# A transformer block with attention and MLP: other homes for the input tiles, other engine for a tile's statistics, and a finer first projection

## The chip, the core and the metric

The kernel runs on one core of a Trainium2 chip. The core has a matrix engine (TensorE, PE in the profile), a vector engine (VectorE, DVE), a scalar engine for activations (ScalarE, ACT), a general one (GpSimd, POOL) and a queue engine (SyncE, SP) from which this kernel issues all of its DMAs. On-chip memory is SBUF; TensorE writes into PSUM, eight banks of which hold 512 fp32 values in each of 128 partitions. The metric is the device time of one execution in microseconds (us). The kernel before took 1038.02 us in the median of three runs (1036.59 to 1038.26).

## The reference

The input x has 2048 rows of 1024 values (bf16). With xn = layernorm(x), the output is x + s * g, where s is an attention block on xn (32 heads of 32, no mask, no second layernorm) and g = silu of an MLP on xn that begins with a layernorm of its own:

```
xn = _layernorm(x, axis=-1)
s = _A_ref(xn, A_wqkv, A_wo)          # qkv = xn @ wqkv; softmax(q k^T / sqrt(32)) v; @ wo
g = _silu(_B_ref(xn, B_w1, B_b1, B_w2, B_b2))   # layernorm, @ w1 + b1, gelu, @ w2 + b2  (F = 3584)
return x + s * g
```

## The kernel before

**Tiling.** x is cut into 16 tiles of 128 rows, x0 to x15. Heads are taken in 8 groups of four (hg 0 to 7). For a group, queries are cut into 8 blocks of 256 (qb) and keys into 8 pairs of 128 (kp, 256 keys). One *unit* (`unit`, L830) is one (qb, kp): eight score matmuls (line L846, called S here), then two exps on ScalarE of 128x1024 values each (L855), then the products with V. 512 units make 1024 exps' worth of work, 1004 of them in the trace's main group. The MLP, the projections and the output product run on TensorE between the units.

**A planner writes the order.** Every operation is declared with its engine, an estimated duration, a priority and what it reads and writes. `_Plan.run` then plays the engines against each other with those estimates and fixes one order for each engine; `settle` adds the semaphore waits. On the chip each engine goes through its list strictly in order, so an instruction that waits holds up everything behind it on its engine. The planner's estimate of a DMA has one common bandwidth queue for SP. Among ready operations of an engine the smaller (priority, index) goes first. In one stretch of planned time, 60 to 90 us, a seed adds noise to some of these choices; the noise depends on the operation's index and on the time.

**The prologue** (first 60 us). For each tile: load (`load_x`, L626, on SP), statistics, rstd, normalised bf16 copy (`normalize`, L748, on DVE), and transposition into xnT, which the projections read.

- Statistics on DVE are two `bn_stats` of 512 values (L785), a `bn_aggr` (L787) and an add of eps (L792). For tile 1 (`AT = 1`) ScalarE does them in place of DVE, with two passes of 1024 values with accumulation (L769), followed by three tiny DVE operations (L772, L774, L777). rstd is a power on POOL (L794), one for each of tiles 0 to 3 and one for each later pair.
- Tiles 0 to 3 are transposed by TensorE (`tr_item`, L733) and copied out of PSUM by ScalarE (L737). Tiles 4 to 15 are transposed by DMA (L752, `DMA_TRANSPOSE xnT<-gw`), issued from SP.
- The normalised copies use four buffers in turn (xnb, in the trace `gw`). The loaded tiles use ten buffers (`NXS = 10`, in the trace `hT`): x0 to x9 are loaded at the start, x10 to x15 only after an earlier tile of the same buffer has been normalised. On SP their loads stand between the DMA transposes.
- The projections of head group 0 are `q_item(n)` and `k_item(n)`, one for each pair of tiles (2n, 2n+1): eight matmuls of 256 columns (L617), and a copy out of PSUM (Q by DVE, L712; K by ScalarE, L722). The first units need Q(0) and K(0); the order of the first units (`order0`) is (0,0), (0,1), (1,0), (1,1), (0,2), (1,2), (2,0), (2,1), (0,3) and so on, so four units, eight exps, can run with tiles 0 to 3, and the ninth exp needs K(2), that is tiles 4 and 5. Head group 0's V follows from `v_item` with the weights wv.
- While TensorE waits, the planner lets it run small matmuls on the identity (`filler`, L668).

Tile numbers t4, t5 and so on below mean the DMA transposes of those tiles.

## Time and profile before

| | us |
|---|---|
| median of three runs | 1038.02 |
| profiled execution, its own time | 1038.8 |
| span of the profiled execution, first to last instruction | 1037.0 |
| ScalarE busy | 1017.2 (98%) |
| TensorE busy | 1000.8 (97%) |
| VectorE busy | 940.6 (91%) |
| start of the first exp | 13.26 |
| last exp ends | 1026.3 |

The profiled time is 0.8 us above the median; 1.8 us of it lie outside the span. Busy times are sums of instruction durations; a TensorE that is busy need not be at its peak. An instruction's row ends in brackets with the idle time of its engine just before it and with what ended that idle time.

### The profile page before, as it was taken

The numbers are of one execution on the slowest core, as the hardware profiler recorded it, in microseconds if no ns is written. First come the engines' busy times: TensorE is split into PE (matmuls) and PEld (weight loads), VectorE is DVE, ScalarE is ACT, GpSimd is POOL, SyncE is SP. The second block draws the span as 40 slices with busy tenths as digits, with TensorE's granted clock in tenths as the row PEclk, the third lists the DMA queues.
The fourth block names the chain that finished last, engine by engine and source line by source line (L and its number), as shares of the span: only waits on it lengthen the run. The fifth ranks groups of instructions, "written<-read, shape, count | busy, mean of one in ns | idle before, by whom it ended". The sixth has DMA issues, their size and how long they took to land.

```text
span 1037.0 us, 31480 instructions
## 1 busy us (share of the span) xinstructions
PE 1000.8 (97%) x14096; PEld 638.6 (62%) x14161; DVE 940.6 (91%) x1308; ACT 1017.2 (98%) x1094; POOL 11.5 (1%) x21
## 2 busy tenths in 40 slices
PE   8999999999999999999999999999999999899997
PEld 6656557666766567666666676666666665664443
DVE  7658999999889999997899989998999889877898
ACT  6999999999999999999999999999999999999996
POOL 2200000000000000000000000000000000000000
PEclk9999999999999999999999999999999999999999
DMA  7994655635665658456447576565365762784421
GB/s 204 166 234 118 173 166 165 191 108 147 192 186 167 168 152 227 129 147 194 136 129 189 146 215 172 159 179 161 104 160 161 212 175 70 230 249 137 135 79 52
DMA packets 318199, 167.99 MB, mean 162 GB/s; under 512 B 56688, under 2 KB 306032, under 8 KB 318064
## 3 DMA queue, kind: packets, MB, share of 16 engines
q1 hardware_dynamic: 318064, 165.98, 58.0%
q8 instruction: 111, 1.82, 0.8%
q14 instruction: 24, 0.20, 0.1%
HBM read 146.55 MB, written 12.06 MB: 153 GB/s over the span
## 4 chain that ended last, share of the span: by engine, by line
ACT 85%; PE 10%; DMA 2%; DVE 2%; issue 1%; SPq 0%; POOL 0%
ACT P L855 78%; PE ps L617 6%; ACT ut L1037 5%; PE ps L612 3%; PE ps L846 2%; DMA xnT<-gw 1%; ACT gw L1064 1%; DMA w2r<-in_B_w_dram 1%; DVE stats L785 1%; DMA hT<-in_A_x_dram 0%; DVE gw L748 0%; DVE hT L1293 0%; DVE V L690 0%; DVE hT L1287 0%; DVE mv L787 0%
## 5 line engine op out<-in xcount | busy, mean ns | idle before, releaser
L855 ACT ACTIVATE P<-ps 128x1024 bf16<-128x1024 f32 x1004 | 937.4, 1236 | 3.6 <-PE ps L846 3.4
L872 DVE TENSOR_TENSOR PA<-P 128x2048 bf16<-128x2048 bf16 x175 | 212.3, 1216 | 38.3 <-ACT P L855 37.7
L617 PE MATMUL ps<-yT,w1r 128*128 128x256 bf16 x1792 | 228.5, 273 | 1.0 <-DVE hT L1022 0.7
L617 PE MATMUL ps<-w2r,hT 128*128 128x256 bf16 x1792 | 223.2, 273 | 0.5 <-DMA w2r<-in_B_w_dram 0.2
L846 PE MATMUL ps<-QKT 32*128 32x256 bf16 x4096 | 203.3, 273 | 13.8 <-ACT P L855 10.9
L886 DVE TENSOR_TENSOR PR<-PR,PA 128x2048 bf16<-128x2048 bf16 x175 | 211.6, 1210 | 1.2
L617 PEld LDWEIGHTS ps<-yT,w1r 128*128 128x128 bf16 x1792 | 164.1, 98 | 54.5 <-issue 29.3
L617 PEld LDWEIGHTS ps<-w2r,hT 128*128 128x128 bf16 x1792 | 163.4, 98 | 50.0 <-issue 31.3
L846 PEld LDWEIGHTS ps<-QKT 32*128 32x128 bf16 x4096 | 60.7, 92 | 144.3 <-ACT P L855 137.3
L612 PE MATMUL ps<-P,V 128*32 128x256 bf16 x4016 | 137.2, 274 | 0.3 <-issue 0.3
L617 PE MATMUL ps<-xnT,wqk 128*128 128x512 bf16 (+1 forms) x511 | 119.1, 360 | 6.5 <-DMA xnT<-gw 2.4
L612 PEld LDWEIGHTS ps<-P,V 128*32 128x32 bf16 x4016 | 95.0, 96 | 31.8 <-issue 22.5
L617 PE MATMUL ps<-wv,xnT 128*128 128x256 bf16 (+1 forms) x576 | 87.1, 285 | 0.5 <-DMA xnT<-gw 0.2
L617 PEld LDWEIGHTS ps<-xnT,wqk 128*128 128x128 bf16 x560 | 49.6, 98 | 53.3 <-issue 14.1
L1022 DVE TENSOR_TENSOR hT<-ps,b1T 128x512 bf16<-128x512 f32 x112 | 76.5, 683 | 1.8 <-PE ps L617 1.1
L872 DVE TENSOR_TENSOR PR<-P 128x2048 bf16<-128x2048 bf16 x61 | 74.1, 1214 | 0.4 <-ACT P L855 0.2
L617 PEld LDWEIGHTS ps<-wv,xnT 128*128 128x128 bf16 x576 | 52.4, 98 | 24.1 <-issue 11.4
L1037 ACT ACTIVATE ut<-ut 128x2048 bf16<-128x2048 bf16 (+1 forms) x32 | 61.0, 1906 | 0.0
L702 DVE CAST QKT<-ps 128x512 bf16<-128x512 f32 x58 | 39.6, 683 | 1.3 <-PE ps L617 0.9
L941 DVE STREAM_TRANSPOSE nt<-ps 128x256 f32<-128x256 f32 x64 | 28.4, 443 | 12.7 <-PE ps L612 12.5
L1039 DVE TENSOR_TENSOR hT<-ut,hT 128x2048 bf16<-128x2048 bf16 (+1 forms) x32 | 34.5, 1079 | 0.2
L1034 DVE TENSOR_TENSOR ut<-hT 128x2048 bf16<-128x2048 bf16 (+1 forms) x32 | 34.5, 1079 | 0.1
(96 smaller groups left out, 549.5 us busy)
## 6 DMA issues: line engine op xcount, KB each, us to landing
w1r<-in_B_w_dram SPq DMA_DIRECT2D x112, 512.0 KB, 4.2
w2r<-in_B_w_dram SPq DMA_DIRECT2D x128, 448.0 KB, 4.6
hT<-in_A_x_dram SPq DMA_DIRECT2D x20, 256.0 KB, 3.9
wqk<-in_A_wqkv_dram SPq DMA_DIRECT2D x16, 256.0 KB, 3.9
yst<-in_A_x_dram SPq DMA_DIRECT2D x16, 256.0 KB, 4.4
g_scratch<-gw SPq DMA_DIRECT2D x32, 128.0 KB, 3.9
o_scratch<-ot SPq DMA_DIRECT2D x56, 64.0 KB, 3.4
xnT<-o_scratch SPq DMA_DIRECT2D x7, 512.0 KB, 6.6
```

The costliest lines, as they stand in the source:

```text
L612: ins = e.matmul(dst(j), lhsT=lhsT(j), rhs=rhs(j), start=start, stop=stop, tile_position=(0, 32 * j), skip_group_check=True)
L617: return e.matmul(dst, lhsT=lhsT, rhs=rhs, start=start, stop=stop, skip_group_check=True)
L702: dve(lambda e: e.tensor_copy(QKT[sl][:, which, tq * 512:(tq + 1) * 512], bank(it.bank)), c_ps(512), [], [(nm, sl, 2 * tq), (nm, sl, 2 * t ...
L846: ins = e.matmul(bank(b0[j], kk * 256, (kk + 1) * 256), lhsT=QKT[sl][32 * j:32 * j + 32, 1, kb * 128:(kb + 1) * 128], rhs=QKT[sl][32 * j:3 ...
L855: x = act(lambda e, h=h: e.activation(Pt[pi][:, 2 * h:2 * h + 2].rearrange("p j k q -> p (j k q)"), ps[:, pr[h] * 1024:(pr[h] + 1) * 1024] ...
L872: return dve(lambda e: e.tensor_tensor(dst[:].rearrange("p u j q -> p (u j) q"), src[:].rearrange("p u j k q -> p (u j) k q")[:, :, 0, :], ...
L886: return dve(lambda e: e.tensor_tensor(fl3(pr), fl3(pr), fl3(PA[i]), op=ALU.add), c_b16(2048), [("PA", i), tok], [tok], 3.2)
L941: dve(lambda e: e.transpose(nt_t[:], bank(pv.bank, 256, 512)), c_ps(256) + 120, [], [("nt",)], prio, pv)
L1022: dve(lambda e: e.tensor_tensor(hT[:, hs], bank(it.bank).rearrange("p (k t) -> p k t", k=2), b1T[:, 2 * pi:2 * pi + 2].unsqueeze(2).to_bro ...
L1034: dve(lambda e: e.tensor_tensor(u_, x_, x_, op=ALU.mult), c_b16(n), hs_, [("ut", ui)], 3)
L1037: act(lambda e: e.activation(u_, u_, ACT.Tanh, scale=GC), c_acts(n), [("ut", ui)], [("ut", ui)], 1)
L1039: dve(lambda e: e.tensor_tensor(x_, u_, x_, op=ALU.mult), c_b16(n), [("ut", ui)] + hs_, hs_, 3)
```

## The change

All sixteen x tiles get homes of their own: x10 to x13 in the two PR buffers, x14 and x15 in the two yst buffers, both idle that early. All sixteen loads are issued one after another, right behind the first weights and ahead of wv. ScalarE takes the statistics of tile 3 too (`AT = (1, 3)`). Q(0) and K(0) are computed by one item, `qk_first`, in halves of 128 columns: first everything of tile 0, then tile 1 in two halves of the contraction, since tile 1's copy out of PSUM comes in two halves; K's half of it lands in PSUM bank 1. K(1) is cut into halves of 128 columns as well. While `qk_first` is open and waits, the planner may put a TensorE transposition between its matmuls; fillers are not planned while an item is open. The first load of the next head group's K weights now waits for the normalisation of tile 15 in place of tile 9; the MLP's first input loads, into yst, wait until tiles 14 and 15 have been normalised, in place of tile 11.

```diff
-        NTR, NWARM, NG0, AT = 4, 8, 3, 1
+        NTR, NWARM, NG0, AT = 4, 8, 3, (1, 3)
...
         xst = [h_flat[:, i * 1024:(i + 1) * 1024] for i in range(NXS)]
+        for i in range(2):
+            pr_flat = PR[i][:].rearrange("p u j q -> p (u j q)")
+            xst += [pr_flat[:, 0:1024], pr_flat[:, 1024:2048]]
+        xst += [yst_t[i][:] for i in range(2)]
...
-        XS = lambda t: ("xst", t % NXS)
+        XS = lambda t: ("xst", t)
...
         wk0 = load_qk(0, 1)
         wq0 = load_qk(0, 0)
-        for t in range(4, NXS):
+        for t in range(NTR, NT):
             load_x(t)
         load_v(0)
...
         def k_item(n):
             it = _Item("pro", 0.01 * n)
-            for dc in range(DC):
+            for lo, w in ((0, 128), (128, 128)) if n < 2 else ((0, 256),):
+                for dc in range(DC):
...
+        def qk_first():
+            it = _Item("pro", -0.001)
+            for lo, d0, d1 in ((0, 0, 8), (128, 0, 4), (128, 4, 8)):
+                for k, wi in ((0, wq0), (1, wk0)):
+                    for dc in range(d0, d1):
+                        def fn(e, b, dc=dc, lo=lo, k=k, wi=wi):
+                            return mm(e, bank(k or b, lo, lo + 128), wqk[wi][:, dc, :], xnT[:, dc, lo:lo + 128],
+                                      dc == 0 and lo == 0, dc == DC - 1)
+                        chunk(it, fn, Q128, [("xnT", lo // 128, dc), ("wqk", wi)], [("S", 0, 1)] if k else ())
...
-                if ts == (AT,):
+                if ts[0] in AT:
+                    a_ = ts[0]
                     for k, f, sc in ((0, ACT.Copy, 1.0 / D), (1, ACT.Square, D ** -0.5)):
...
-                    if t >= NXS:
-                        load_x(t, [first[2 * n - 5]])
...
-            wk = load_qk(hg, 1, [first[9]] if hg == 1 else ())
+            wk = load_qk(hg, 1, [first[NT - 1]] if hg == 1 else ())
...
-                    [("yst", t2)], rate=390.0, extra=[first[11]] if c == 0 else ())
+                    [("yst", t2)], rate=390.0)
...
+        for i in range(2):
+            after([("PR", i)], [XS(10 + 2 * i), XS(11 + 2 * i)])
+            after([("yst", i)], [XS(14 + i)])
```

In the planner, `pe_step` gets the rule for the inserted transposition:

```diff
+            tq, th = self.dense["tr"], heads["tr"]
+            if use is None and S["do"] is not None and th < len(tq) and tq[th].chunks[0].left == 0 and tq[th].chunks[0].ready <= t:
+                heads["tr"] += 1
+                tq[th].k = 1
+                S["mode"] = "d"
+                commit(tq[th].chunks[0], t)
+                return
```

More of the change, by code (lines that the diff above doesn't have):

```diff
@@ L13 @@
 ENGS = ("PE", "ACT", "DVE", "POOL", "SP")
-Q256, Q512 = 109.0, 216.0
+Q128, Q256, Q512 = 58.0, 109.0, 216.0
 SWITCH = {"dr": 104.0, "rd": 98.0, "vr": 112.0, "rv": 96.0, "dv": 102.0, "vd": 115.0}
@@ L625, in load_x @@
         def load_x(t, extra=()):
-            dma(f"x{t}", lambda e: e.dma_start(xst[t % NXS], x2[t * 128:(t + 1) * 128, :]), 262144, [], [XS(t)],
+            dma(f"x{t}", lambda e: e.dma_start(xst[t], x2[t * 128:(t + 1) * 128, :]), 262144, [], [XS(t)],
                 rate=390.0, prio=2, occ=500, lat=2450, extra=extra)
@@ L717, in k_item, with fn @@
             it = _Item("pro", 0.01 * n)
-            for dc in range(DC):
-                def fn(e, b, dc=dc):
-                    return mm(e, bank(b, 0, 256), wqk[wk0][:, dc, :], xnT[:, dc, n * 256:(n + 1) * 256], dc == 0, dc == DC - 1)
-                chunk(it, fn, Q256, [("xnT", 2 * n, dc), ("xnT", 2 * n + 1, dc), ("wqk", wk0)])
+            for lo, w in ((0, 128), (128, 128)) if n < 2 else ((0, 256),):
+                for dc in range(DC):
+                    def fn(e, b, dc=dc, lo=lo, w=w):
+                        at = n * 256 + lo
+                        return mm(e, bank(b, lo, lo + w), wqk[wk0][:, dc, :], xnT[:, dc, at:at + w], dc == 0 and lo == 0, dc == DC - 1)
+                    chunk(it, fn, Q256 if w == 256 else Q128, [("xnT", 2 * n + i, dc) for i in range(lo // 128, (lo + w) // 128)] + [("wqk", wk0)])
             act(lambda e: e.activation(QKT[0][:, 1, n * 256:(n + 1) * 256], bank(it.bank, 0, 256), ACT.Copy), c_act(256), [],
                 [("K", 0, n)], -1, it)
+            return it
+        def qk_first():
[7 more added lines that the diff above has]
+                        chunk(it, fn, Q128, [("xnT", lo // 128, dc), ("wqk", wi)], [("S", 0, 1)] if k else ())
+            dve(lambda e: e.tensor_copy(QKT[0][:, 0, 0:256], bank(it.bank, 0, 256)), c_ps(256), [], [("Q", 0, 0)], 0, it)
+            act(lambda e: e.activation(QKT[0][:, 1, 0:256], bank(1, 0, 256), ACT.Copy), c_act(256), [("S", 0, 1)], [("K", 0, 0)], -1)
             return it
@@ L747, in normalize @@
         def normalize(t, rs):
-            first[t] = dve(lambda e: e.tensor_scalar(xnb[t % 4], xst[t % NXS], mv[:, t, 0:1], lnp[:, t, 1:2],
+            first[t] = dve(lambda e: e.tensor_scalar(xnb[t % 4], xst[t], mv[:, t, 0:1], lnp[:, t, 1:2],
                                           op0=ALU.subtract, op1=ALU.mult), c_b4(1024) + 118,
@@ L766, in bass_recurrent_scan__mha_block__mixer_channel_mlp__prompt_kernel @@
             for ts in groups:
-                if ts == (AT,):
+                if ts[0] in AT:
+                    a_ = ts[0]
                     for k, f, sc in ((0, ACT.Copy, 1.0 / D), (1, ACT.Square, D ** -0.5)):
-                        act(lambda e, k=k, f=f, sc=sc: e.activation(
-                            fl3(PA[0])[:, k * 1024:(k + 1) * 1024], xst[AT], f, scale=sc, accum_out=mv[:, AT, k:k + 1]),
-                            c_acts(1024) + 93, [XS(AT)], [("st", AT, k)], 1)
-                    dve(lambda e: e.tensor_tensor(lnp[:, AT:AT + 1, 2], mv[:, AT:AT + 1, 0], mv[:, AT:AT + 1, 0], op=ALU.mult), 65,
-                        [("st", AT, 0)], [("s2",)], 0.95)
-                    dve(lambda e: e.scalar_tensor_tensor(lnp[:, AT:AT + 1, 0], mv[:, AT:AT + 1, 1], EPS, lnp[:, AT:AT + 1, 2], op0=ALU.add,
-                                                         op1=ALU.subtract), 65,
-                        [("st", AT, 1), ("s2",)], [("ve", AT)], 0.95)
-                    dve(lambda e: e.tensor_tensor(mv[:, AT:AT + 1, 1], mv[:, AT:AT + 1, 1], lnp[:, AT:AT + 1, 2], op=ALU.subtract), 65,
-                        [("st", AT, 1), ("s2",)], [("mv", AT)], 1.1)
+                        act(lambda e, k=k, f=f, sc=sc, a_=a_: e.activation(
+                            fl3(PA[a_ // 2])[:, k * 1024:(k + 1) * 1024], xst[a_], f, scale=sc, accum_out=mv[:, a_, k:k + 1]),
+                            c_acts(1024) + 93, [XS(a_)], [("st", a_, k)], 1)
+                    dve(lambda e, a_=a_: e.tensor_tensor(lnp[:, a_:a_ + 1, 2], mv[:, a_:a_ + 1, 0], mv[:, a_:a_ + 1, 0], op=ALU.mult), 65,
+                        [("st", a_, 0)], [("s2", a_)], 0.95)
+                    dve(lambda e, a_=a_: e.scalar_tensor_tensor(lnp[:, a_:a_ + 1, 0], mv[:, a_:a_ + 1, 1], EPS, lnp[:, a_:a_ + 1, 2],
+                                                                op0=ALU.add, op1=ALU.subtract), 65,
+                        [("st", a_, 1), ("s2", a_)], [("ve", a_)], 0.95)
+                    dve(lambda e, a_=a_: e.tensor_tensor(mv[:, a_:a_ + 1, 1], mv[:, a_:a_ + 1, 1], lnp[:, a_:a_ + 1, 2], op=ALU.subtract),
+                        65, [("st", a_, 1), ("s2", a_)], [("mv", a_)], 1.1)
@@ L779, in bass_recurrent_scan__mha_block__mixer_channel_mlp__prompt_kernel @@
                 for t in ts:
-                    if t == AT:
+                    if t in AT:
                         continue
-                    if t >= NXS:
-                        load_x(t, [first[2 * n - 5]])
                     for c in range(2):
-                        dve(lambda e, t=t, c=c: e.bn_stats(stats[:, t, c, :], xst[t % NXS][:, c * 512:(c + 1) * 512]),
+                        dve(lambda e, t=t, c=c: e.bn_stats(stats[:, t, c, :], xst[t][:, c * 512:(c + 1) * 512]),
                             605, [XS(t)], [("st", t, c)], 1.2)
@@ L790, in bass_recurrent_scan__mha_block__mixer_channel_mlp__prompt_kernel @@
                 rs = ("rs", lo)
-                if ts != (AT,):
+                if ts[0] not in AT:
                     dve(lambda e, lo=lo, hi=hi: e.tensor_scalar_add(lnp[:, lo:hi, 0], mv[:, lo:hi, 1], EPS), 80,
@@ L799, in bass_recurrent_scan__mha_block__mixer_channel_mlp__prompt_kernel @@
                 plan.dense["tr"] += [tr_item(2 * n), tr_item(2 * n + 1)]
-            if n < NG0:
-                pro_q.append(q_item(n))
-            pro_q.append(k_item(n))
+            if n == 0:
+                pro_q.append(qk_first())
+            else:
+                if n < NG0:
+                    pro_q.append(q_item(n))
+                pro_q.append(k_item(n))
             pro_q.sort(key=lambda it: it.pos)
@@ L816, in bass_recurrent_scan__mha_block__mixer_channel_mlp__prompt_kernel @@
         pool(lambda e: e.tensor_tensor(lnp[:, :, 2], mv[:, :, 1], lnp[:, :, 1], op=ALU.mult), 250,
-             rss + [("mv", t) for t in range(NT)], [("s2",)], 2)
+             rss + [("mv", t) for t in range(NT)], [("s2",), ("s2", AT[0]), ("s2", AT[1])], 2)
         pool(lambda e: e.tensor_tensor(lnp[:, :, 2], lnp[:, :, 2], lnp[:, :, 1], op=ALU.mult), 250, [("s2",)], [("s2",)], 2)
```

## The prediction

> **What bounds the kernel now.** I read the page first, for the engines' shares and the costliest group:

> ```profile
> PE 1000.8 (97%) x14096; PEld 638.6 (62%) x14161; DVE 940.6 (91%) x1308; ACT 1017.2 (98%) x1094; POOL 11.5 (1%) x21
> L855 ACT ACTIVATE P<-ps 128x1024 bf16<-128x1024 f32 x1004 | 937.4, 1236 | 3.6 <-PE ps L846 3.4
> ```

> ScalarE is the bound, and nearly all of it is exps. A share over the whole span hides where its 20 us of idle time lie, so next came the busy time of ScalarE alone in stretches that I cut at the first exp, the ninth exp and the last:

> ```profile
> 0.00:13.26 13.26, 7.16 (x12) 1.00 0.90 264
> 13.26:24.28 11.02, 9.14 (x12) 1.00 0.53 138
> 24.28:60.00 35.72, 34.59 (x42) 1.00 0.99 175
> 60.00:80.00 20.00, 18.54 (x21) 1.00 0.85 241
> 80.00:1026.30 946.30, 946.22 (x1009) 1.00 0.57 160
> 1026.30:1037.00 10.70, 1.57 (x3) 0.81 0.21 74
> ```

> The columns are stretch, length, busy us and count, granted clock, DMA share, GB/s. From 80 us to the last exp ScalarE is idle for 0.08 us. So a microsecond saved on its path before 80 us comes off the end, and nothing else does. To be had there: 1.88 us between exp 1 and exp 9, 1.13 up to 60, 1.46 up to 80. Idle time before the first exp counts only if exp 9 moves with it. The timeline shows what ended the larger waits:

> ```profile
> 23.07 0.38 ACT L722 ACTIVATE QKT<-ps 128x256 bf16<-128x256 f32 x1 [1.15 <-PE ps L617]
> 38.67 1.02 ACT L855 ACTIVATE P<-ps 128x1024 bf16<-128x1024 f32 x1 [0.92 <-PE ps L846]
> 21.98 1.70 PE L617 MATMUL ps<-xnT,wqk 128*128 128x256 bf16 x14 [1.30 <-DMA xnT<-gw]
> 37.91 0.38 PE L617 MATMUL ps<-xnT,wqk 128*128 128x256 bf16 x2 [1.07 <-DMA xnT<-gw]
> ```

> Both come from a DMA transpose: t5 for K(2) at 21.98, t11 for K(5) at 37.91. (The second is an accident of order: the exp at 38.67 doesn't need K(5), but its S stands behind K(5)'s first matmuls on TensorE.) The chain in order of time says what set t4 and t5, the first exp having no part in it:

> ```profile
> 14.90 0.72 POOL lnp L794
> 15.64 1.00 DVE gw L748 x2
> 16.64 0.96 DVE stats L785 x2
> 17.61 4.33 DMA xnT<-gw
> 21.98 1.06 PE ps L617 x8
> ```

> (The 0.96 is SP busy with t4's issue.) Back from 14.90 it is an unbroken run of DVE statistics to x2's landing at 6.00. So two things set K(2): DVE's queue, then the DMA. Last, the DMA's load in stretches (same columns with all engines, DMA share and GB/s at the end), and issue-to-landing of t10 alone and of t6 alone:

> ```profile
> 8.00:14.00 6.00, 5.63 (x83) 4.75 (x81) 5.85 (x15) 4.17 (x6) 1.33 (x2) 1.00 1.05 335
> 14.00:17.00 3.00, 2.96 (x43) 2.35 (x40) 2.70 (x7) 2.50 (x4) 0.71 (x1) 1.00 0.02 5
> xnT<-gw SPq DMA_TRANSPOSE x1, 6.8
> xnT<-gw SPq DMA_TRANSPOSE x1, 2.7
> ```

> The first loads keep the DMA engines full until 14.0, then they idle for 3 us until t4. t6 was issued into an empty queue, t10 behind the loads of x12 to x15.

> **The change part by part.** *Tile 3's statistics.* DVE loses two `bn_stats` at 0.61, a `bn_aggr` at 0.22 and an add at 0.15 (1.6 us) and gains three tiny operations (0.14, 0.07, 0.07): 1.3 less. Tile 2's copy then waits some 0.4 for POOL's rstd (8.48 + 0.78), which tile 3's statistics cover today. Net 1.0 (bounds 0.6 and 1.3): t4's copy starts at about 14.6 in place of 15.64, its issue at 15.2 in place of 16.21.

> ScalarE gains two passes of 1.05, 2.1 us. x3 lands at 2.11 + 4.7 = 6.8, so pass one fits into the 1.45 idle before 7.95; pass two stands between tile 0's copy (ends 8.9) and tile 1's (9.58 today) and delays that by 0.4. All of it lies ahead of K(2), for which ScalarE waits anyway: cost 0. Without that cover it would cost the full 2.1.

> *`qk_first`.* Today 16 matmuls of 256 columns (0.11 apart) run from 10.42 and K(0)'s copy starts at 12.37. Now tile 0's 16 halves run before tile 1 arrives, and after tile 1's last copy (10.9 with the delay) only 8 halves of 0.06 remain, 0.5: K(0)'s copy at about 11.8, first exp at 12.7, or 13.1 if tile 3's copy out of PSUM (1.02, between the first two exps today) goes first. Gain 0.2 to 0.6, worth 0 at the end: exps 1 to 8 are done by about 21.3 (13.1 + 8 x 0.93, K(1)'s copy 0.3, a gap of 0.5 as today) and exp 9 waits for K(2). The 3 fillers of this stretch that fall away cost nothing; the granted clock stays 1.00 even where TensorE idles for 0.98 us, at 21 to 22. K(1) in halves: the same columns, 0.

> *The loads.* On SP six loads (1.05 at 18.94 and 2.00 at 27.92) leave their places between transposes and go behind x9. At 0.48 each they put wv's issue from 8.97 to 11.9; SP then still idles until 15.2, and wv's first matmul is at 25.66: cost 0 on SP. In the DMA engines they are 6 x 262,144 B = 1.57 MB; at 335 GB/s that is 4.7 us, at the 353 GB/s of 10 to 13 us 4.5. The burst ends at 18.6 in place of 14.0. It fills the gap, and t4 and t5 now stand behind it. This is the disputed price:

> - No cost: t4 and t5 behave like t6 and t7 (issues at 21.89 and 23.19, the latter landing 2.8 later at 25.98: 4.1 for the pair). From 15.2 that is 19.3, 2.6 earlier than the 21.93 of today.
> - In turn, at an empty queue's speed: t6's bytes start at about 23.0, the pair has landed 3.0 later, 2.6 without the pause between them. From 18.6 that is 21.2 to 21.6; I take 21.3, 0.6 earlier.
> - Like t10 and t11: issue at 30.21, both landed at 31.57 + 6.24 = 37.81, 7.6 later. From 15.2 that is 22.8, 0.9 later.

> I take the middle, -0.6: t10 shows that a transpose waits its turn, and its row has other disturbances in it (loads of wqk and yst behind it, none here). ScalarE follows one to one: K(2)'s matmuls and copy, exp 8, exp 9. The lower end is -2.4, since exps 1 to 8 must be done.

> [...]

> *Later tiles.* Without x12 to x15 ahead of them t10 and t11 should land as t6 did. DVE's run from t5's copy (16.6) to t10's (29.64) takes 13 us with 2.3 of waits in it; starting 1.0 earlier it puts t10's issue near 29, both landed by 33, against 36.8 when TensorE comes to them. The 0.92 at 38.67 goes. What is late next: K(6) and K(7), landed at 42.3 and 48.2, where ScalarE shows 0.2 of idle time in 40 to 60; DVE, off its loads, brings them earlier too. Ends: -0.92 and 0.

> *The next K weights and the first MLP inputs* wait for tiles 15, 14 and 15: from 34.41 and 35.04 to the end of t15's copy, 43.2 today. The weights serve head group 1, 64 units of two exps (0.93 each) on. The MLP's inputs, which land 3.8 and 4.7 after issue, would be there by 47.9, and their copy today starts at 47.0; it waits for POOL's chain behind tile 15 (45.08 + 0.22) in any case. The whole moves ahead with DVE: cost 0.

> *The rest of the order.* All lists behind are planned anew. The 1.46 us at 60 to 80 are two waits of TensorE for nothing that the profile shows (0.99 and 0.88) under a DMA share of 0.85. They may go (-1.46), stay, or be joined by two more of the size 0.9 (+1.8). I take 0.

> **Sum:** -0.6 - 0.92 = -1.5 us. Profiled execution: 1038.8 - 1.5 = 1037.3. The median lies 0.8 below that execution, so 1038.0 - 1.5 = **1036.5**. Ends: -2.4 - 0.92 - 1.46 = -4.8 and 0.9 + 0 + 1.8 = +2.7.

> **Rivals.** *A, further ahead:* the transposes slip into gaps of the burst, or the stretch at 60 to 80 clears. For it: t4 landed in 2.9 with little around it, and the MLP's start spreads out. Against: t10. 1 to 2.5 us beyond the forecast, out of the 2.0 more on t5 and the 1.46: 1035.5 to 1034.0.

> [...]

> *C, slower:* the new order stalls S between 60 and 100 us. It is the one stretch where the plan holds a seed's noise, keyed by indices that the change shifts, and where ScalarE ran dry already (1.46). Each stall like the two there costs 0.9. Two more (+1.8) cancel the gain; from four more (-1.5 + 3.6 = +2.1) it is slower by 0.2%: 1040. For it: TensorE is 97% busy and follows a fixed list. Against: from 80 to 1026 the same kind of list left 0.08 idle.

> **How the numbers follow.** 0.2% (2.1 us) is about what a measurement of this kernel tells from no change, half more than the spread of the three runs. The forecast gets 0.40, with a range of its own from 1035.6 to 1037.4; three tenths of it pass the line (0.12 faster, 0.28 same). A 0.28, faster. B 0.10, same. C 0.22, slower. So faster 0.40, same 0.38, slower 0.22. The range reaches into A and C, to 1034.0 and 1040.2.

> **What would show it.** t4 issued near 15.2, the DMA engines full until 18.6, t5 landed near 21.3, exp 9 near 23.7 in place of 24.28; no wait near 37 to 39; still 1.5 idle at 60 to 80. The forecast is wrong if t5 lands beyond 22.8 or before 20, if ScalarE's passes delay exp 8 past K(2), or if ScalarE is idle for more than 0.5 us anywhere after 80.

## The result, and the profile after

The changed kernel took 1040.54 us in the median of six runs (1039.22 to 1042.59), the kernel before 1038.16 in six (1036.59 to 1040.48). The ratio is 1.0023, with a 95% interval from 1.0014 to 1.0033: slower by 2.4 us, where 1.5 us less were forecast. The profiled execution took 1042.59 us, the longest of the six and 2.0 above their median; its span is 1040.8, 3.8 more than before. So what is read from it below explains these 3.8 us, and not all of it is in the typical execution. The page, engines and costliest group:

```profile
PE 1010.6 (97%) x14171; PEld 640.6 (62%) x14171; DVE 938.9 (90%) x1307; ACT 1018.7 (98%) x1098; POOL 11.7 (1%) x21
L883 ACT ACTIVATE P<-ps 128x1024 bf16<-128x1024 f32 x1004 | 937.4, 1245 | 2.4 <-PE ps L874 2.4
```

The exps take 937.4 us, as before. So the difference is idle time. ScalarE alone in stretches, cut at the first exp (13.19), the ninth exp and the last (columns: stretch, length, busy us and count, granted TensorE clock, DMA share, GB/s):

```profile
13.19:27.76 14.57, 8.10 (x12) 0.84 0.98 194
27.76:60.00 32.24, 29.81 (x36) 0.91 0.70 125
60.00:80.00 20.00, 19.07 (x21) 1.00 0.91 243
80.00:1030.10 950.10, 950.10 (x1014) 1.00 0.57 160
```

From 80 us on nothing is lost, as before. The last exp ends 3.80 us later, and that is made up of: exp 9 at 27.76 in place of 24.28, +3.48; idle time from there to the last exp 2.43 + 0.93 + 0.00 against 1.13 + 1.46 + 0.08, +0.69; 0.37 less work in that part. The granted clock shows something that the kernel before did not: 0.84 and 0.91 ahead of 60 us. The timeline of ScalarE and that of TensorE around it:

```profile
25.92 0.38 ACT L735 ACTIVATE QKT<-ps 128x256 bf16<-128x256 f32 x1 [5.01 <-PE ps L628]
...
27.76 3.77 ACT L883 ACTIVATE P<-ps 128x1024 bf16<-128x1024 f32 x4 [1.46 <-PE ps L874]
...
32.93 1.94 ACT L883 ACTIVATE V<-ps 128x1024 bf16<-128x1024 f32 x2 [1.40 <-PE ps L874]
```

```profile
18.68 0.95 PE L679 MATMUL ps<-ident 128*128 128x128 bf16 x14
23.99 3.17 PE L628 MATMUL ps<-xnT,wqk 128*128 128x256 bf16 x14 [4.35 <-DMA xnT<-gw]
```

The last fillers end at 19.63. Then TensorE has nothing to do for 4.35 us, until t5 has landed; before, it waited 1.30. And the same 14 matmuls of K(2) then take 3.17 us in place of 1.70. The chain in order of time shows where t5's delay comes from, and SP's timeline with it:

```profile
14.35 1.00 DVE gw L774 x2
...
18.24 5.71 DMA xnT<-gw
```

```profile
14.92 3.27 SPq L778 DMA_TRANSPOSE xnT<-gw  x1
```

t4's copies begin at 14.35, 1.3 earlier than before, and t4's issue at 14.92. But SP needs 3.27 us for that one issue (1.34 before, and the same 1.34 in the experiment below where the loads are not ahead of it), so t5 is issued only at 18.24, 0.6 later than before (17.61). From there it takes 5.71 in place of 4.33, which is another 1.4, and it lands at 23.94, 2.0 later than before. What lengthens this second part the trace does not show. Last, all of TensorE in stretches of 3.41 us (same columns as above, for PE):

```profile
19.62:23.03 3.41, 0.02 (x1) 1.00 1.48 160
23.03:26.44 3.41, 2.45 (x12) 0.50 0.53 115
26.44:29.86 3.42, 2.83 (x25) 0.50 0.00 0
29.86:33.27 3.41, 3.41 (x23) 0.50 0.68 154
```

After a stretch in which TensorE was busy for 0.02 us, the granted clock is 0.50 for three such stretches, 10.24 us, and it is back at 1.00 after the third, the one that was busy throughout (3.41 us; the first two 2.45 and 2.83).

### The profile page after: what moved, and what is told of

Read it like the earlier page. It is cut to its first block, busy times and chain, and to the rows that moved or that the text cites. A ratio compares the mean times of both kernels' runs of the same rounds, so it can differ in the third digit from the quotient of the medians.

```text
span 1040.8 us, 31571 instructions
## 1 busy us (share of the span) xinstructions
PE 1010.6 (97%) x14171; PEld 640.6 (62%) x14171; DVE 938.9 (90%) x1307; ACT 1018.7 (98%) x1098; POOL 11.7 (1%) x21
## 3 DMA queue, kind: packets, MB, share of 16 engines
q8 instruction: 111, 1.82, 0.7%
## 4 chain that ended last, share of the span: by engine, by line
ACT 88%; PE 8%; DVE 2%; DMA 1%; issue 0%; POOL 0%; SPq 0%
ACT P L883 80%; PE ps L628 5%; ACT ut L1065 5%; PE ps L623 2%; PE ps L874 2%; ACT gw L1092 1%; DVE stats L810 1%; DMA xnT<-gw 1%; ACT w2r L883 1%; DMA hT<-in_A_x_dram 0%; ACT hT L883 0%; ACT w1r L883 0%; DVE hT L1324 0%; DVE gw L774 0%; ACT V L883 0%
## 5 line engine op out<-in xcount | busy, mean ns | idle before, releaser
L883 ACT ACTIVATE P<-ps 128x1024 bf16<-128x1024 f32 x1004 | 937.4, 1245 | 2.4 <-PE ps L874 2.4
L874 PE MATMUL ps<-QKT 32*128 32x256 bf16 x4096 | 204.1, 274 | 11.5 <-ACT P L883 9.5
L628 PE MATMUL ps<-xnT,wqk 128*128 128x512 bf16 (+2 forms) x584 | 133.3, 358 | 6.6 <-DMA xnT<-gw 4.4
L628 PEld LDWEIGHTS ps<-wv,xnT 128*128 128x128 bf16 x576 | 53.1, 99 | 24.5 <-issue 11.8
L969 DVE STREAM_TRANSPOSE nt<-ps 128x256 f32<-128x256 f32 x64 | 28.4, 444 | 12.2 <-PE ps L623 11.9
```

Of the source, the lines that this page charges most:

```text
L628: return e.matmul(dst, lhsT=lhsT, rhs=rhs, start=start, stop=stop, skip_group_check=True)
L874: ins = e.matmul(bank(b0[j], kk * 256, (kk + 1) * 256), lhsT=QKT[sl][32 * j:32 * j + 32, 1, kb * 128:(kb + 1) * 128], rhs=QKT[sl][32 * j:3 ...
L883: x = act(lambda e, h=h: e.activation(Pt[pi][:, 2 * h:2 * h + 2].rearrange("p j k q -> p (j k q)"), ps[:, pr[h] * 1024:(pr[h] + 1) * 1024] ...
L969: dve(lambda e: e.transpose(nt_t[:], bank(pv.bank, 256, 512)), c_ps(256) + 120, [], [("nt",)], prio, pv)
```

## The experiments

All kernels here compute the whole reference; the fillers that some of them enlarge write nothing that is read. Two theories took shape; the first expectations call the first of them Theory 1. **W**: the loads make t5 late, TensorE idles ahead of K(2), the clock falls, and that is the loss. **F**: TensorE's stalls between 30 and 75 us that no semaphore explains have to do with the DMA queue that the page names "instruction" (111 packets, 1.82 MB, in the kernel before and in the changed one). The author's guess is that its packets bring TensorE's instructions and come late where the DMA engines are full of other transfers (the expectations speak of fetches and of full rings); then the places of the stalls would depend on how many TensorE instructions were issued before, and any edit of the prologue would move them. Medians, with the ratio to the kernel before on the same chip in the same minutes:

| kernel | us | ratio, 95% interval |
|---|---|---|
| changed kernel again | 1041.31 | 1.0037 [1.0022, 1.0051] |
| changed, x10 to x15 loaded late | 1039.67 | 1.0023 [1.0012, 1.0033] |
| before, with homes and loads alone | 1038.69 | 1.0009 [0.9999, 1.0020] |
| changed, fillers 12 x 128 ahead of K(2) | 1038.19 | 1.0004 [0.9995, 1.0013] |
| changed without homes and loads | 1040.04 | 1.0010 [0.9998, 1.0022] |
| the same without `qk_first` and halves | 1043.15 | 1.0042 [1.0029, 1.0056] |
| without homes and loads, fillers 6 x 128 | 1036.34 | 0.9980 [0.9971, 0.9989] |
| changed, loads late, fillers 6 x 128 | 1038.36 | 0.9998 [0.9986, 1.0010] |
| without homes and loads, fillers 2 x 512 | 1039.44 | 1.0019 [1.0008, 1.0029] |
| without homes and loads, fillers 6 x 32 | 1035.85 | 0.9984 [0.9973, 0.9994] |
| changed, fillers 2 x 512 | 1039.97 | 1.0019 [1.0007, 1.0030] |
| before, fillers 6 x 32 | 1037.47 | 0.9997 [0.9988, 1.0005] |
| changed, fillers 6 x 32 well ahead of K(2) | 1040.47 | 1.0024 [1.0015, 1.0033] |
| without homes and loads, four w2 loads put off | 1038.02 | 1.0000 [0.9990, 1.0010] |
| changed, four w2 loads put off | 1041.65 | 1.0035 [1.0023, 1.0047] |
| without homes and loads, fillers 12 x 32 | 1036.91 | 0.9992 [0.9982, 1.0002] |
| before, four w2 loads put off | 1036.99 | 0.9990 [0.9981, 0.9999] |
| fillers 6 x 32 and four w2 loads put off | 1035.70 | 0.9978 [0.9966, 0.9989] |

### The parts, and the clock: first runs

Every kernel has one profile, of one execution, and this execution can lie far from the median; where it does, the text says so. The changed kernel itself, run again beside the others:

> The changed kernel once more, beside the others on one chip: 1.0023 of the kernel before, 2.4 us more. In its profile the granted clock falls to 0.50 at about 23 us, after TensorE has idled for over 3.4 us, and comes back some 10 us later.

1041.31 us. Its profile tells the same story: t5 at about 23.7, exp 9 at 27.50, the clock at 0.50 from 22.33 for 10.24 us, behind 3.41 us in which TensorE was busy for 0.77.

The burst undone, and only it: the homes stay, x10 to x15 are issued where the kernel before issues them.

```diff
-        for t in range(NTR, NT):
+        for t in range(NTR, 10):
             load_x(t)
...
+                    if t >= 10:
+                        load_x(t, [first[2 * n - 5]])
```

> The changed kernel, but x10 to x15 are loaded where the kernel before loads them (own homes, ScalarE's statistics and the finer projections stay). Theory 1 (the burst of loads makes t4 and t5 late, the idle TensorE then loses its clock): t4's issue near 15 takes 1.3 us again, t5 lands by 21, exp 9 starts near 23.0, the clock stays 1.00, and the kernel is faster than before by 1 us (0.9985 to 1.0). Theory 2 (the loss comes from the other parts: two more passes on ScalarE, the halved projections, the new order behind them): still 1.002.

1039.67 us. TensorE's timeline:

```profile
20.72 1.81 PE L628 MATMUL ps<-xnT,wqk 128*128 128x256 bf16 x15 [1.51 <-DMA xnT<-gw]
...
56.73 0.40 PE L623 MATMUL ps<-P,V 128*32 128x256 bf16 x7 [1.66 <-issue]
...
67.20 0.40 PE L623 MATMUL ps<-P,V 128*32 128x256 bf16 x7 [0.95 <-issue]
```

t4's issue takes 1.34, t5 lands at 20.68, and exp 9 starts at 22.91, 1.4 us ahead of the kernel before. So the burst makes t5 some 3 us later than it need be. But the expected gain did not come: at a ratio of 1.0023 the kernel is slower than before, like the changed kernel. In its profile (1038.74 us) two stalls that no semaphore explains cost ScalarE 1.75 and 0.74.

The other half alone, homes and loads in the kernel before (the diff of the change without `AT`, `qk_first` and the halves):

> The kernel before with the loads alone: own homes for all tiles, all loads at once, the same later places for the next K weights and the first MLP inputs. Theory 1: t4 (issued near 16.2) and t5 stand behind the burst as in the changed kernel, t5 lands near 24, 2 us late; the wait of 0.92 at 38 goes. Without a loss of clock +1 us (1.001), with it +3 to +4 (1.003). [...] Theory 2: like before, 1.000 or less.

1038.69 us: t5 lands at 23.22, 1.3 later, and TensorE idles 2.89 us ahead of K(2), but the clock stays at 1.00 (from 13 to 34 us), and the matmuls of K(2) take 1.70. Without the clock's fall, the burst costs 0.9 us by the ratio, and by its interval anything from nothing to 2.1.

The clock alone: the seven fillers that the plan puts at 17.9 to 18.7 us run 12 matmuls each, which lasts until t5 arrives. That keeps TensorE busy, and it also adds 70 matmul instructions.

```diff
-  lambda e, b=bf[1], n=1 if t < 6000.0 else 2: self.filler(e, b, n)
+  lambda e, b=bf[1], n=1 if t < 6000.0 else 12 if 17900.0 < t < 18700.0 else 2: self.filler(e, b, n)
```

> The changed kernel, but the 7 fillers planned last before K(2) run 12 small matmuls each in place of 2, so that TensorE has about 4.9 us of them from 18.7 on and never idles for long; orders and DMAs are unchanged. Theory 1a (most of the loss is the clock, not the late landing itself): t5 still lands near 24, the clock stays 1.00, exp 9 starts at about 26.3 in place of 27.8, the 1.4 us wait at 32.9 goes, and some 2.5 us of time: 0.9995 of the kernel before. Theory 1b (the late landing is all of it): 1.002 still.

1038.19 us, 3.1 less than the changed kernel beside it (3.4 by the ratios), although t5 still lands at about 23.3. TensorE in stretches and the start of exp 9 (all engines: PE, PEld, DVE, ACT, POOL, then clock, DMA share, GB/s; the timeline below it):

```profile
24.00:33.00 9.00, 8.09 (x95) 5.36 (x94) 6.84 (x16) 7.92 (x11) 0.70 (x1) 1.00 0.33 75
```

```profile
25.47 3.77 ACT L883 ACTIVATE P<-ps 128x1024 bf16<-128x1024 f32 x4 [0.62 <-PE ps L874]
```

The clock is 1.00, exp 9 comes at 25.47 in place of 27.76, and the waits of 1.40 at 32.93 and 0.79 at 51.56 are gone. This profile is of the fastest of twelve executions (1036.48 us).

### The change without its loads

All that stands on the loads taken back (homes, loads, what waits for tile 15), so that the statistics on ScalarE and the projections tile by tile remain:

> The changed kernel with the homes and loads of the kernel before (ten buffers, x10 to x15 late, the next K weights and the first MLP inputs at their old places): ScalarE's statistics of tile 3 and the halved first projections remain. Theory 1 (those two are sound, t4 and t5 come 1.3 us earlier): exp 9 at 22.9 as in the run with late loads, 1.4 ahead of before; and since the DMAs behind tile 15 are not pressed together, that is kept: 0.9987, clock 0.998 to 0.999 in nearly all executions. Theory 2 (these two parts cost time or clock themselves, as the spread of the run with late loads suggests): 1.001 or more, with executions at a clock of 0.994 to 0.997.

1040.04 us, with executions from 1036.26 to 1044.30. t5 lands at 21.20 and exp 9 starts at 23.44, yet this kernel is not faster than before. Its profile is of the slowest of twelve executions. Then without `qk_first` and the halves too, so that only tile 3's statistics have moved:

> As the run before it, but the first projections whole, as in the kernel before, so fillers are planned again while tile 1 is awaited: ScalarE's statistics of tile 3 alone. If the halved item's missing fillers cost clock, this one has 0.998 to 0.999 and 0.999 or less of the time, below the run before it. If the halves are harmless: the same as that one within 0.1%, since exp 9 waits for t5 in both.

1043.15 us, the slowest of all, which neither expectation foresaw: t5 at 19.34, K(2) is copied at 21.06, the earliest of all. From 32.70 TensorE waits 2.62 us, here for a later transpose, and the mean clock from 34 to 45 us is 0.84. Three more stalls of 1.3 to 1.5 follow (one waits for DVE, two for nothing that the profile shows); the mean clock of the whole execution is 0.994. Now the version before that one, the one at 1040.04 us, with fillers of six matmuls at 17.9 to 18.7 us:

```diff
+  ... n=1 if t < 6000.0 else 6 if 17900.0 < t < 18700.0 else 2 ...
```

> The two parts without the loads, and the 6 fillers planned last before K(2) run 6 matmuls each in place of 2 (2.1 us of them, until about 20.5, when t5 lands). If lost clock before K(2) makes its executions uneven, the clock is 0.998 to 0.999 in all and the time 0.998 to 0.999 of before; if the clock isn't at stake there, the same as without them.

1036.34 us, faster than both kernels. And the same fillers in the version with the homes and late loads:

> The changed kernel with late loads, with the same longer fillers before K(2). If the clock was lost at K(2) in the slow executions of the run with late loads (1.0023, clock from 0.994), they go: 0.999 to 1.000. If it is lost elsewhere, behind 45 us, where its DMAs stand pressed together and TensorE waited 1.7 us for nothing that the profile shows: 1.002 again.

1038.36 us; its profile has a stall of 2.10 at 54.97 that no semaphore explains, and the mean clock is 0.94 from 45 to 60 us and 0.96 from 60 to 80.

Why the fillers helped was not what W says. Without the loads t5 comes early, and the clock is 1.00 up to 34 us in the profiles of both versions. Theory F looks at the number of TensorE instructions instead. TensorE's and ScalarE's timelines of the version at 1040.04 us show the worst of these stalls, and the last line the DMA's queue of instructions from 67 to 71 us (packets, MB, share of 16 engines; the row DMA is the busy share in 40 slices, in tenths):

```profile
70.88 0.40 PE L619 MATMUL ps<-P,V 128*32 128x256 bf16 x7 [3.34 <-issue]
```

```profile
72.09 1.94 ACT L881 ACTIVATE P<-ps 128x1024 bf16<-128x1024 f32 x2 [3.42 <-PE ps L872]
```

```profile
DMA  9999999999999999999999999999999999999999
...
q8 instruction: 1, 0.02, 1.8%
```

TensorE stands from 67.54 to 70.88. From 67 to 71 us one packet of the instruction queue, 16 KB, passes, while the DMA engines are full (share 1.19 from 66 to 72 us) with w2 loads, issued from 62.21 on, that take 7.8 us each to land.

The profiles of the kernel before and of the changed one show the same nearness. Between 24 and 1030 us they hold three stalls of TensorE of 0.3 us or more that no semaphore explains, ending at 63.46 and 68.56 (before) and at 72.37 (changed), and these end 1.40, 1.42 and 1.40 us after the end of an instruction packet. Whose instructions the packets hold the profile does not say. That they are TensorE's is an inference from their spacing: in these two traces a packet starts every 255 or 256 TensorE instructions (matmuls and weight loads) in the mean, and from a line of that slope the packets scatter by 0.15 of one spacing; counted in ScalarE's instructions the scatter is 0.29 of a spacing, in VectorE's 0.47.

### Warmth against the number of instructions

Four kernels separate the two. The same fillers as two matmuls of 512 columns: warm, and no more instructions than without them.

```diff
+  ins = e.matmul(bank(b, 0, 512), lhsT=ident[:], rhs=xnT[:, 0, 0:512], ...)   # 2 of these in place of 2 of 128
```

> The kernel with the loads of before, the statistics on ScalarE and the first pair's projections tile by tile (1040.04 us, clock .996 in its profile); its six dropped fillers before K(2) come back as two matmuls of 512 columns each: the same number of TensorE instructions as without them, about 2.6 us more TensorE work at 18 to 21 us. Theory W (what counts is that TensorE works in the 3.41 us before K(2)): as with the six times six small ones, 1036.0 to 1037.0 us. Theory F (what counts is where TensorE's instruction fetches fall, and the 48 extra instructions only moved them): as without them, 1039 to 1041 us, with TensorE gaps of over 1.5 us that no semaphore explains between 32 and 75 us.

1039.44 us: no gain. (Its profile, of the fastest of eleven executions, has stalls of 0.74 and 0.68 only.) As six matmuls of 32 columns: the instructions, hardly any work.

> The same kernel with the six fillers as six matmuls of 32 columns each: the number of TensorE instructions of the 1036.34 us version, but only about 1 us of TensorE work before K(2). Theory F: 1036.0 to 1037.0 us, no TensorE gap over 1 us after 24 us that no semaphore explains. Theory W: 1038.5 to 1040.5 us, and a half clock in some profiles.

1035.85 us: the whole gain, with no stall of TensorE of 0.3 or more between 24 and 80 us that no semaphore explains in its profile (the fastest of eleven executions). In this version it is the number that counts, as F has it. The changed kernel with the wide fillers:

> The changed kernel with its seven fillers before K(2) as two matmuls of 512 columns each: number of TensorE instructions as in the changed kernel, about 3 us more TensorE work between 18.7 and 22 us. Theory W: the clock stays 1.00 from 22 to 34 us, the 14 matmuls of K(2) take 1.7 us instead of 3.17, exp 9 starts near 25.5 us instead of 27.8, and the time falls by 2 to 3 us to 1038 to 1039 us. Theory F: the clock in that stretch stays up as well, but TensorE's fetch gaps stay where they are in the changed kernel, and the time falls by less than 1 us, to 1040 to 1041 us.

1039.97 us. ScalarE's timeline:

```profile
25.48 3.77 ACT L886 ACTIVATE P<-ps 128x1024 bf16<-128x1024 f32 x4 [0.62 <-PE ps L877]
```

The stage is mended as with the 12 small ones (exp 9 at 25.48; of the wait of 0.79 a wait of 0.52 is left), but the ratio falls only from 1.0023 and 1.0037, the two measurements of the changed kernel, to 1.0019, with an interval that overlaps both. So warmth alone is not shown to make the kernel faster, and the gain of the 12 small matmuls cannot be put down to warmth alone. The executions split: eight have a mean clock of 0.998 or 0.999 (1037.3 to 1041.4 us), four of 0.994 to 0.996 (1040.1 to 1042.5), so in some of them the clock falls elsewhere; the profiled one is of the first kind, and the fastest (1037.31). The kernel before with fillers as six of 32:

> The kernel before with its fillers planned for 17.9 to 18.7 us as six matmuls of 32 columns instead of two of 128: about the same TensorE time, some more instructions, so that nothing but the places of TensorE's later instruction fetches is moved. Theory W: as before, within 0.7 us (1037.5 to 1039 us). Theory F: moved by 1 to 3 us either way, with TensorE gaps at other places than before's in 30 to 80 us.

1037.47 us, not to be told from before. The stalls do move (1.14 and 0.52, ending at 56.73 and 66.93, in place of 0.99 and 0.88 at 63.46 and 68.56), but they add up to about the same.

### DMA engines emptied, and the number alone

The changed kernel with eight fillers at 14.6 to 15.4 us as six matmuls of 32 columns: more instructions, nothing more in the 3.41 us before K(2).

> The changed kernel with eight fillers planned at 14.6 to 15.4 us as six matmuls of 32 columns each instead of two of 128: 32 more TensorE matmuls well ahead of K(2), nothing more in the 3.41 us before it. Theory F (places of TensorE's instruction fetches): the clock still falls to one half near 23 us, and the time still falls by 1.5 to 3 us, to 1037.5 to 1039 us. Theory W (the clock before K(2)): no gain, 1040 to 1042 us.

1040.47 us: no gain. In the changed kernel this number alone does nothing, as W has it. The profiled execution took 1039.15, and shows one way in which executions differ. TensorE in stretches of 3.41 us:

```profile
20.56:23.97 3.41, 0.37 (x4) 1.00 0.93 137
23.97:27.38 3.41, 3.41 (x23) 0.50 0.26 59
27.38:30.79 3.41, 2.81 (x35) 1.00 0.34 77
```

t5 arrived at 23.6, and the clock fell at 23.97. The 3.41 us at half clock were busy throughout, and behind them the clock was back at 1.00, after 3.41 us in place of 10.24.

The test of the full DMA engines: the first four w2 loads (1.8 MB, first used after 150 us) each wait for a later S, planned for 81 to 92 us, where they stood at 57 to 62. Order and number of all other instructions stay.

```diff
+        late = [o for o in plan.ops if o.eng == "SP" and o.sem[:2] == "w2"][:4]
+        for i, o in enumerate(late):
+            d = plan.s_queue[36 + 2 * i]
+            o.deps[d] = True
+            d.users.append(o)
+            o.left += 1
         plan.run()
```

In the version without homes and loads:

> The kernel with the loads of before, the statistics on ScalarE and the projections tile by tile (1040.04 us), with the four first w2 loads (1.8 MB, first used at 150 us) put off from 57 to 62 us to four points between 81 and 92 us; order of all other work and number of TensorE instructions unchanged. Theory F with full DMA rings as the cause of a late fetch: the stall near 67 to 71 us goes, ScalarE is busy for over 19.5 of the 20 us from 60 to 80, time 1037 to 1038.5 us. If the number of instructions acts in another way than by fetches behind full rings: unchanged, 1039 to 1041 us.

1038.02 us. By the ratios that is 1.0 less (1.0000 after 1.0010), and the intervals overlap. The DMA's view from 63 to 66 us, where an instruction packet now passes ahead of the matmul that stalled above:

```profile
DMA  9999999999999842111111100000111111100000
...
q8 instruction: 1, 0.02, 2.5%
```

This packet passes in the 3 us in which the DMA engines empty, where the one above passed between 67 and 71 us, and the stall ahead of the same matmul is 0.33 in place of 3.34. (The 3.34 is from the slowest of twelve executions.) In the changed kernel:

> The same deferral of the four w2 loads in the changed kernel. Theory F: only its stalls behind 65 us go (0.93 us of ScalarE idle time from 60 to 80 us in its profile), the half clock at 23 us stays: 1039.0 to 1040.3 us against 1040.5. Otherwise unchanged, 1040 to 1042 us.

1041.65 us: ScalarE is busy for all of the 20 us from 60 to 80, but the clock is at 0.50 from 23.50 for 10.24 us, and nothing is gained. Its few stalls are not where the changed kernel loses. Twelve matmuls of 32 columns in place of six, in the version without homes and loads:

> The kernel with the loads of before, the statistics on ScalarE and the projections tile by tile, its six fillers as twelve matmuls of 32 columns instead of six (1035.85 us with six): 36 more matmuls again. Theory F: the time depends on where the fetches fall and not steadily on the count; anywhere from 1035.5 to 1040 us, and the fetches seen at 31, 40 and 52 us with six come another 2 to 4 us earlier. Theory W: more TensorE work before K(2) can't hurt, 1035.5 to 1036.5 us.

1036.91 us, between the others: its profile has a stall of 1.80 again, which ends at 65.02. The time does not change steadily with the count (1040.04, 1035.85, 1036.91).

Last, the emptier DMA engines in the kernel before, and in the fastest version:

> The kernel before with the four first w2 loads put off from 57 to 62 us to 81 to 92 us, nothing else. If the kernel before also loses to late instruction fetches there (ScalarE idle 1.46 us from 60 to 80 us in its profile): 1036.4 to 1037.4 us, and the gain of the fastest version is for the most part that of fewer stalls. If not: 1037.6 to 1038.3 us, and the gain is that of the statistics and the projections.

> The version without the new loads, with six fillers of six matmuls of 32 columns (1035.85 us), and the same deferral. It has no ScalarE idle time left from 60 to 80 us in its profile: if stalls there come in other executions, they go and the time falls to 1035.0 to 1035.6 us; if not, 1035.6 to 1036.5 us.

1036.99 and 1035.70 us. The kernel before gains 1.2 us by it too (0.1 to 2.0 by the interval). The rest of the way to 1035.70, 1.3 us, is small against the noise (the intervals overlap); the statistics on ScalarE, the projections tile by tile and the added matmuls can all have a share in it, and the runs do not part these three. This last kernel, without the change's loads, beats both (ratio 0.9978 [0.9966, 0.9989] to before).

### What the clock costs, from the executions themselves

Every execution comes with its mean granted clock. The changed kernel and its two versions that keep the fall (32-column fillers, w2 loads put off) have 36 executions in all, and none is above 0.997; the two versions that are kept warm have 17 of 24 at 0.998 or 0.999, as nearly all of the kernel before.

| mean clock | the fall kept: executions, median us | kept warm: executions, median us |
|---|---|---|
| 0.992 | 1, 1045.4 | 0 |
| 0.993 | 11, 1041.9 | 0 |
| 0.994 | 2, 1040.7 | 1, 1041.8 |
| 0.995 | 5, 1040.9 | 1, 1040.1 |
| 0.996 | 10, 1040.2 | 3, 1041.9 |
| 0.997 | 7, 1039.2 | 2, 1039.6 |
| 0.998 | 0 | 11, 1038.4 |
| 0.999 | 0 | 6, 1037.5 |

0.993 is the profile with 10.24 us at half clock, 0.997 the one with 3.41: 2.7 us of time between them, some 1.35 for each stretch of 3.41. By that the median execution of the changed kernel (about 0.996, between one stretch and two) loses some 2 us to the clock, most of the 2.4; this is an estimate from the table, not a run of its own. It may be too high, since a long stall of TensorE can make an execution longer and lower its mean clock as well: in the slowest execution of the version at 1040.04 us a stall of 3.34 us was followed by 3.41 us at 0.50, from 71.42 on.

## Why the prediction was wrong

**What bounds the kernel** held: idle time of ScalarE ahead of 80 us, and nothing after it.

**Tile 3's statistics** held: t4's copies at 14.35 (14.6 forecast), its issue at 14.92 (15.2). **ScalarE's passes and `qk_first`** held: exps 1 to 8 were done by 20.9 (21.3), first exp 13.19 (13.1), and no exp waited for a pass.

**The loads** is one step that failed, by its size and beyond its bound. I took t5 at 21.3, between 19.3 and 22.8; it landed at 23.94. I had modelled the wait for the bytes (in turn behind the burst, at an empty queue's speed) and left out that the issue itself is held. SP sat 3.27 us in t4's issue, so t5 was issued 3.3 us after t4, and then took 5.71 us to land. The run with the loads undone (t5 at 20.68, t4's issue 1.34, 4.68 from t5's issue to its landing) shows that the loads do both. In the profiled execution that is 2.6 us of the miss. With the clock kept up it is worth less at the end: homes and loads in the kernel before cost 0.9 by the ratio.

**"The 3 fillers of this stretch that fall away cost nothing; the granted clock stays 1.00 even where TensorE idles for 0.98 us"** is the other step that failed, and in the profiled execution it and t5 turned the sign. It was read off an idle time of 0.98, and the changed kernel has one of 4.35: late t5 behind fillers that the list had used up by 19.63. The clock fell to 0.50. K(2) took 1.47 longer, and the waits at 32.93 and 51.56 (1.40 and 0.79) came with it; both are absent where the 12 small matmuls keep the clock up, while with the wide fillers 0.52 of the second stays. In the profiled execution this sums up with t5 to the miss of 5.3 us (span 1035.5 forecast, 1040.8 measured): 2.64 for t5 and 1.47 for K(2), less 0.05, make exp 9 late, and behind exp 9 2.2 more idle time up to 60, 0.5 less to 80 and 0.45 less of work and waits. I costed the missing fillers from a row with a short idle time and did not ask what a long one does to the clock.

What the profiles show of a longer one: the clock fell behind 3.41 us in which TensorE was busy for 0.02 us (changed kernel), 0.77 (the same again) and 0.37 (32-column fillers well ahead of K(2)), and it was at 0.50 for 10.24, 10.24 and 3.41 us. Each time it was back at 1.00 behind 3.41 us that were busy throughout; behind the stretches that were busy for 2.45 and 2.83 us, and for 2.00 and 2.83, it stayed at 0.50. In the kernel before with homes and loads alone an idle time of 2.89 us left it at 1.00. From how little work on it falls was not measured.

**Later tiles** held: the wait of 0.92 at 38.67 is gone. **The rest of the order**, taken at 0, came out at 0.5 less from 60 to 80. One smaller slip: 2.1 us is not half more than the spread of the three runs (1.67 us) but a quarter more.

**The rivals.** C had the sign with a chance of 0.22, but not the mechanism: it looked for new stalls at 60 to 100 us, and the profile of the changed kernel has 0.93 us there. Such stalls are real, though, and in the profiles they are what took back the gain of the rest of the change: without the loads exp 9 started 0.84 us earlier than before, and the version was still no faster (1.0010). With the w2 loads put off it came out level (1.0000), and only with another instruction count was it faster (0.9984). B (t4 and t5 as late as t10 and t11, 0.9 later for t5) had the right direction, and t5 went further, 2.0 later. The signal that I had named for a wrong forecast, t5 beyond 22.8, is what came.

**What stays open.** That t5 comes late and that the clock falls is shown; how much of the 2.4 us the two cost together is not. Taking the loads back alone brought nothing (1.0023), as stalls stood elsewhere. The share of the clock lies between 0.4 us (wide fillers against the nearer of the two measurements) and 3.4 (small fillers, in the same minutes, which also added 70 matmuls); the clocks of the executions put it at 2. That a late fetch of instructions is what stalls TensorE was not shown. The guess rests on the packets' ends 1.40 to 1.42 us ahead of the ends of three stalls, on the packets' spacing, on the times with other numbers of instructions, and on the earlier packet where the DMA engines are emptier; a request for a packet is not in the trace. Where the clock falls in the executions of the warm versions that have a mean under 0.997 was not seen, as each kernel has one profile.

## What to carry to other kernels

When a change delays a transfer that TensorE waits for, look at the granted clock as well as at the wait: here, behind 3.41 us in which TensorE was busy for 0.02 to 0.77 us, the work that followed ran at 0.50 of the clock for 3.41 to 10.24 us, and the matmuls of K(2) took 3.17 us in place of 1.70. Both lengths were seen for nearly the same work: 10.24 us in two profiles of the changed kernel, 3.41 in that of its version with 32-column fillers. Look at the issuing engine too when loads are put ahead of a critical DMA on its queue: here t4's issue took SP 3.27 us in place of 1.34, and t5, behind it, was issued at 18.24 in place of 17.61. And before a variant of the prologue is believed to be better or worse by 0.2%, shift the number of TensorE instructions ahead of the loaded stretch: that alone moved one version of this kernel by some 3 us, and left two others where they were.
